# Dilated attention on one core: numerators and sums written in token order, sums first, fewer bias masks

## The chip, the cores and the metric

One core of a Trainium2 chip. The metric is the device time of one execution in microseconds. The kernel before takes 363.38 us (median of 3 runs, 363.35 to 364.58). "PE" is the tensor engine, "DVE" the vector engine, "ACT" the scalar engine, "POOL" GpSimd. PSUM is the memory of the tile `ps`, which the matmuls of every view below write to; the kernel lays it out as eight banks of 512 fp32 columns.

## The reference

Attention over 8 batches, 8 heads, 576 tokens, 64 columns a head. Heads 0 to 3 see a plain window of 32 tokens; heads 4 to 7 a dilated one, every fourth token back to 128. Then a gated feed-forward layer.

```python
rel = pos[:, None] - pos[None, :]
mask_plain = (rel >= 0) & (rel < 32)
mask_dil = (rel >= 0) & (rel < 32 * 4) & (rel % 4 == 0)
scores = np.where(masks, scale * q @ k.T, -1e9)
attn = softmax(scores)            # the kernel divides by the sums after attn @ v
x = (attn @ v)                    # to [4608 tokens, 512]
out = (gelu(x @ w_gate) * (x @ w_val)) @ w_out
```

## The kernel before

Work comes in 32 "units" of two heads: unit n is batch n // 4; n % 4 of 0 and 1 are plain, 2 and 3 dilated. The feed-forward layer runs in 9 blocks of 512 tokens, and the attention of later batches is placed between its matmuls by a list of places. Batches 2 (units 8 to 11) and 3 (12 to 15) are worked off within the output matmuls of blocks 1 and 2. In the dilated heads a token is 4i + 2m + s; the kernel keeps each class (m, s) apart.

```python
def emit_pv(n, b0, parts=("num", "den"), wide=False):
    ...                                        # dilated unit:
    for s in range(2):                         # numerators
        for m in range(3):
            for hl in range(2):
                h, p0 = 2 * hp + hl, (2 * s + hl) * DW
                if m < 2:
                    add(hl, 512 * s + m * NCL, run(P), vd[:, h, 2 * m + s, :], p0 + m * NCL, run(P), m == 0)
                else:
                    two = [[NCL, 2], [1, 16]]
                    add(hl, 512 * s + P, two, vr[:, h, s, :], p0 + P, two, False)
    ...                                        # sums: matmuls with ones, 192/96/96/192 columns (narrow), 288/288 (wide)

def norm_r(n, b0, wide=False):                 # DVE: transpose of the sums, reciprocal, transpose back
def norm_x(n, b0):                             # DVE: xT = numerators * reciprocals
    num = ps[:, b0 : b0 + 2, 0 : 2 * NCL].rearrange("p s (m i) -> p i m s", m=2)
    nc.vector.tensor_tensor(dst.rearrange("p (i m s) -> p i m s", m=2, s=2), num,
                            rb.rearrange("p (s m i) -> p i m s", s=2, m=2), ALU.mult)

def emit_s(n, b0, pe_mask=False):              # scores and exponential; if pe_mask, PE first adds a bias of -60000
    ...                                        # (4 matmuls) where the mask is 0; else DVE multiplies by the mask after
biased = (6, 7, 8, 9, 10, 11, 12, 13, 14, 15)
four = "1.5s 1.9v 1.12s 2.6v 2.12s 3.3v 3.12s 3.12v"   # places in blocks 1 and 2: tile.matmul, s = scores, v = values

def pv(last):                                  # what a "v" does
    n = todo.pop(0)
    emit_pv(n, V)                              # V: one set of three PSUM banks
    if not last:
        mask_next()                            # DVE mask of the NEXT unit, ahead of ...
    norm(n, V)                                 # ... the normalisation of this one
```

"Narrow" units (values within output matmuls) have three PSUM banks for numerators and sums together; "wide" ones have two for each.

The softmax here doesn't subtract the row's maximum and nothing guards it: scores larger than these inputs give would overflow.

## Time and profile before

| | before |
|---|---|
| time, median | 363.38 us |
| PE busy | 345.5 of a span of 362.5 us |
| DVE busy | 184.8 us |
| PE waits for DVE's products of dilated units (value matmuls + first feed-forward matmuls) | 2.0 + 1.6 us |
| product of a dilated unit / plain unit | 1126 / 745 ns |

The prediction below shows the lines that carry this. The chain that ended last (start us, length us, what) gives the length of a whole piece on PE: the bias of a plain unit (L323), of a dilated one (L346), and the numerators and sums of a narrow dilated unit (unit 18, 20 matmuls) and of a wide dilated one (unit 26, 16 matmuls):

```profile
94.97 0.57 PE ps L323 x4
98.37 0.49 PE ps L346 x4
181.76 0.66 PE ps L433 x20
238.43 0.65 PE ps L433 x16
```

The groups by line, for the numerators of the dilated units (busy us, mean ns | idle before):

```profile
L433 PE MATMUL ps<-P,vd 128*64 128x128 f16 x128 | 6.8, 224 | 2.0 <-DVE xT L469 2.0
L433 PE MATMUL ps<-P,vr 128*64 128x32 f16 x64 | 5.2, 179 | 0.0
```

A mean of 224 ns is the length of one pipelined matmul, not its cost: in the timeline of unit 10, printed in the prediction, two run side by side, in the two halves of the array (128*64 each, where a feed-forward matmul is 128*128): the 1152 columns of its numerators take 0.30 us (104.30 to 104.60), where one after the other they would make 0.48 at the 0.42 ns a column of a 512-column matmul (0.216 us). Four of 128 columns take 0.13 and 0.11 us there from their start to that of the next group, two of 32 columns 0.03 us. What a matmul costs is read from the start of one to the start of the next.

### The profile page before, as it was taken

Reading aid. Unit: us, or ns where it says so; the run is one execution under the profiler, and the core shown is the slowest. Engines: PE = TensorE matmul, PEld = TensorE weight load, DVE = VectorE, ACT = ScalarE, POOL = GpSimd, SP = SyncE. Lnnn points to the kernel's source line nnn. Section 1 sums busy time; section 2 is a strip of 40 time slices with the busy share of each in tenths; the row PEclk is TensorE's granted clock in tenths of the full one; section 3 lists DMA queues with packets and bytes.
Section 4 is the critical chain, followed back from the end, with each engine's and each line's share of the span. In section 5 each row is a group of like instructions: output and inputs, shape, how many; then the busy total and the mean of one; then the engine's idle time right before and its main releaser. Section 6 shows DMA issues by size and latency. Waiting matters only on the chain.

```text
span 362.5 us, 6061 instructions
## 1 busy us (share of the span) xinstructions
PE 345.5 (95%) x2400; PEld 164.2 (45%) x2400; DVE 184.8 (51%) x278; ACT 146.0 (40%) x212; POOL 78.2 (22%) x110
## 2 busy tenths in 40 slices
PE   7879899999989999899999999999999999999995
PEld 2554354444544445444444444444444444444442
DVE  1585445744266325864477638783669413303320
ACT  1733255253543345434553356336542223312321
POOL 2580333540432332063003410240000000000000
PEclk9899999999999999999999999999999999999999
DMA  7999999999899898599438962893100030011002
GB/s 184 244 177 214 220 133 194 192 157 235 188 142 204 181 161 154 136 173 135 101 93 186 158 96 89 195 140 72 60 30 2 0 116 2 1 60 58 0 29 89
DMA packets 107292, 45.31 MB, mean 125 GB/s; under 512 B 83040, under 2 KB 102496, under 8 KB 107264
## 3 DMA queue, kind: packets, MB, share of 16 engines
q1 hardware_dynamic: 84272, 31.21, 39.8%
q0 software_dynamic: 21456, 12.01, 26.6%
q10 hardware_dynamic: 1536, 1.70, 2.0%
q8 instruction: 19, 0.31, 0.4%
q14 instruction: 9, 0.07, 0.1%
HBM read 40.13 MB, written 9.44 MB: 137 GB/s over the span
## 4 chain that ended last, share of the span: by engine, by line
PE 78%; DMA 13%; DVE 5%; POOL 2%; ACT 1%; issue 1%; ACTq 0%; SPq 0%; POOLq 0%; DVEq 0%
PE ps L481 41%; PE ps L512 25%; PE ps L433 5%; DMA xT<-in_k_dram 4%; DMA st<-in_k_dram 3%; PE ps L493 3%; DMA wv<-in_moe_w_val_dram 3%; DMA wo<-in_moe_w_out_dram 2%; DVE xT L469 2%; PE ps L360 1%; DMA sv<-in_v_dram 1%; PE ps L330 1%; DVE dt L451 1%; DVE rb L455 1%; PE ps L346 1%; POOL qp L251 1%
## 5 line engine op out<-in xcount | busy, mean ns | idle before, releaser
L506 DVE SCALAR_TENSOR_TENSOR u_all<-g,ps 128x512 f16<-128x512 f16 x108 | 73.5, 686 | 85.9 <-PE ps L481 76.9
L505 ACT ACTIVATE g<-ps 128x512 f16<-128x512 f32 x108 | 63.6, 597 | 126.0 <-PE ps L481 115.0
L512 PE MATMUL ps<-wo,u_all 128*128 128x512 f16 x432 | 101.1, 380 | 1.1 <-DMA wo<-in_moe_w_out_dram 0.7
L481 PE MATMUL ps<-xT,wg 128*128 128x512 f16 x392 | 100.7, 379 | 0.3
L481 PE MATMUL ps<-xT,wv 128*128 128x512 f16 x392 | 100.6, 379 | 0.0
L512 PEld LDWEIGHTS <-u_all 128*128 128x128 f16 x432 | 39.2, 98 | 45.4 <-issue 1.5
L481 PEld LDWEIGHTS <-wv 128*128 128x128 f16 x392 | 38.4, 98 | 46.4 <-issue 0.2
L481 PEld LDWEIGHTS <-wg 128*128 128x128 f16 x392 | 37.2, 98 | 45.0 <-issue 2.1
L523 ACT ACTIVATE osb<-ps 128x512 f32<-128x512 f32 x33 | 19.7, 597 | 49.0 <-PE ps L512 49.0
L451 DVE STREAM_TRANSPOSE dt<-ps 128x576 f32<-128x576 f32 x32 | 24.9, 779 | 26.2 <-PE ps L433 25.9
L190 POOL CAST qp<-st 128x2048 f16<-128x2048 f32 x6 | 11.4, 1894 | 99.0 <-DMA st<-in_k_dram 84.8
L455 DVE STREAM_TRANSPOSE rb<-rc 128x576 f32<-128x576 f32 x32 | 24.9, 778 | 1.1
L362 ACT ACTIVATE P<-ps 128x1152 f16<-128x1152 f32 x16 | 18.1, 1130 | 10.8 <-PE ps L360 10.8
L340 ACT ACTIVATE P<-ps 128x960 f16<-128x960 f32 x16 | 15.5, 970 | 10.7 <-PE ps L330 10.6
L469 DVE TENSOR_TENSOR xT<-ps,rb 128x576 f16<-128x576 f32 x16 | 17.9, 1126 | 0.3
L493 PE MATMUL ps<-xT,wg 128*128 128x512 f16 x40 | 15.2, 379 | 2.1 <-DVE xT L469 1.6
L525 DVE TENSOR_SCALAR osb<-ps 128x512 f32<-128x512 f32 x3 | 2.1, 691 | 28.8 <-PE ps L512 28.8
L433 PE MATMUL ps<-P,ones 128*64 128x96 f16 (+5 forms) x216 | 14.3, 245 | 1.6 <-ACT P L362 1.6
L493 PE MATMUL ps<-xT,wv 128*128 128x512 f16 x40 | 15.2, 379 | 0.0
L466 DVE TENSOR_TENSOR xT<-ps,rb 128x576 f16<-128x576 f32 x16 | 11.8, 745 | 0.3
L370 DVE TENSOR_TENSOR P<-P,mask_p 128x1344 f16<-128x1344 f16 x10 | 8.4, 852 | 6.8 <-ACT P L341 6.8
L370 DVE TENSOR_TENSOR P<-P,mask_d 128x1152 f16<-128x1152 f16 x8 | 6.1, 757 | 11.1 <-ACT P L362 11.1
(75 smaller groups left out, 244.2 us busy)
## 6 DMA issues: line engine op xcount, KB each, us to landing
out_dram<-osb SPq DMA_DIRECT2D x36, 256.0 KB, 2.1
sv<-in_v_dram SPq DMA_DIRECT2D x40, 128.0 KB, 3.2
st<-in_q_dram SPq DMA_DIRECT2D x24, 128.0 KB, 3.7
st<-in_k_dram SPq DMA_DIRECT2D x24, 128.0 KB, 3.1
qd<-in_q_dram POOLq DMA_DIRECT2D x7, 256.0 KB, 5.0
qd<-in_k_dram POOLq DMA_DIRECT2D x7, 256.0 KB, 6.9
vd<-in_v_dram POOLq DMA_DIRECT2D x7, 256.0 KB, 7.2
wg<-in_moe_w_gate_dram POOLq DMA_DIRECT2D x3, 512.0 KB, 7.4
```

Of the source, the lines that this page charges most:

```text
L340: nc.scalar.activation(pt[:, :, 0:PB], sb[:, 0, :, 0:PB], AF.Exp, bias=0.0, scale=scale)
L362: nc.scalar.activation(pt, ps[:, b0 : b0 + 4, 0:DW], AF.Exp, bias=0.0, scale=scale)
L433: nc.tensor.matmul(o, lhs, rhs, start=st, stop=True, skip_group_check=True)
L451: nc.vector.transpose(dst, den)
L455: nc.vector.transpose(rb.rearrange("p (b c) -> p b c", c=32), bass.AP(tensor=rc.tensor, offset=rc.offset, ap=[rc.ap[0], [1, 18], [0, 32]]),)
L469: nc.vector.tensor_tensor(dst.rearrange("p (i m s) -> p i m s", m=2, s=2), num, rb.rearrange("p (s m i) -> p i m s", s=2, m=2), ALU.mult,)
L481: nc.tensor.matmul(ps[:, b0 + gi, :], w[:, kc, ns], xT[kc][:, tok], start=(kc == 0), stop=(kc == NKC - 1))
L493: nc.tensor.matmul(ps[:, pairs[nb] + gi, :], w[:, kc, ns], xT[kc][:, tok], start=(kc == 0), stop=(kc == NKC - 1),)
L505: nc.scalar.activation(g, ps[:, b0, :], AF.Gelu)
L506: nc.vector.scalar_tensor_tensor(u_all[:, nb, :], g, USCALE, ps[:, b0 + 1, :], ALU.mult, ALU.mult)
L512: nc.tensor.matmul(ps[:, bank, :], u_all[:, fc, tb * P : (tb + 1) * P], wo_t[fc // 4][:, fc % 4, :], start=(fc == 0), stop=(fc == NNB - 1),)
L523: nc.scalar.activation(osb, ps[:, bank, :], AF.Copy, bias=0.0, scale=1.0 / USCALE)
```

## The change

The intent is to relieve DVE: PE writes numerators and sums of dilated units straight in token order, so that DVE's product reads in order. With the DVE time won, six of ten bias masks move from PE to DVE, and the sums are issued before the numerators so that DVE can begin earlier.

```diff
-    def emit_pv(n, b0, parts=("num", "den"), wide=False):
+    def emit_pv(n, b0, parts=("den", "num"), wide=False):
 ...  # sums now ahead of numerators; dilated sums, for s in 0, 1:
-                    else ((0, 0, 192, 288), (0, 192, 96, 800), (1, 0, 96, 896), (1, 96, 192, 1312))
+                    for i0, i1 in ((0, P),) if wide else ((0, 16), (16, P)):
+                            add(hl, d0 + 4 * i0 + s, [[2, 2], [4, i1 - i0]], ones, p0, [[NCL, 2], [1, i1 - i0]], s == 0)
+                        add(hl, d0 + 512 + s, [[2, 2], [4, 16]], ones, p0, two, s == 0 and wide)
 ...  # dilated numerators
-            add(hl, 512 * s + m * NCL, run(P), vd[:, h, 2 * m + s, :], p0 + m * NCL, run(P), m == 0)
+            add(hl, 2 * m + s, [[4, P]], lhs, p0, run(P), m == 0 and s == 0)
-            add(hl, 512 * s + P, two, vr[:, h, s, :], p0 + P, two, False)
+            add(hl, 512 + s, [[2, 2], [4, 16]], vr[:, h, s, :], p0 + P, two, s == 0)
 ...  # product, all units
+        nc.vector.tensor_tensor(xT[hp][:, b * S : (b + 1) * S], psf[:, b0 * 512 : b0 * 512 + S], rb, ALU.mult)
-    biased = (6, 7, 8, 9, 10, 11, 12, 13, 14, 15)
-    four = "1.5s 1.9v 1.12s 2.6v 2.12s 3.3v 3.12s 3.12v"
+    biased = (6, 7, 8, 12)
+    four = "1.5s 1.6v 1.12s 2.4v 2.12s 3.3v 3.12s 3.12v"
```

An access pattern `[[4, P]]` means P elements, each four fp32 (16 bytes) from the last.

More of the change, by code (lines that the diff above doesn't have):

```diff
@@ L390, in run @@
             return [[1, n]]
+        two = [[NCL, 2], [1, 16]]
+        d0 = 1024 if wide else 960
         if is_plain(n):
-            if "num" in parts:
-                for j in range(5):
-                    for hl in range(2):
-                        lhs = vp[:, j, 2 * hp + hl, :] if j < 4 else vt[:, 2 * hp + hl, :]
-                        w = (PW, PW, PW, P, PT)[j]
-                        add(hl, j * P, run(w), lhs, hl * PH + j * PW - (32 if j == 4 else 0), run(w), j in (0, 4))
             if "den" in parts:
-                d0 = 1024 if wide else 960
                 groups = (
@@ L410, in emit_pv @@
                         add(hl, d0 + q0, [[P, runs], [1, w]], ones[:, 0:D], hl * PH + p0, [[PW, runs], [1, w]], st)
-        else:
+            if "num" in parts:
+                for j in range(5):
+                    for hl in range(2):
+                        lhs = vp[:, j, 2 * hp + hl, :] if j < 4 else vt[:, 2 * hp + hl, :]
+                        w = (PW, PW, PW, P, PT)[j]
+                        add(hl, j * P, run(w), lhs, hl * PH + j * PW - (32 if j == 4 else 0), run(w), j in (0, 4))
+        else:
+            if "den" in parts:
+                for s in range(2):
+                    for i0, i1 in ((0, P),) if wide else ((0, 16), (16, P)):
+                        for hl in range(2):
+                            dims = [[2, 2], [4, i1 - i0]]
+                            p0 = (2 * s + hl) * DW + i0
+                            add(hl, d0 + 4 * i0 + s, dims, ones[:, 0:D], p0, [[NCL, 2], [1, i1 - i0]], s == 0)
+                    for hl in range(2):
+                        p0 = (2 * s + hl) * DW + P
+                        add(hl, d0 + 512 + s, [[2, 2], [4, 16]], ones[:, 0:D], p0, two, s == 0 and wide)
             if "num" in parts:
@@ L417, in emit_pv @@
                             if m < 2:
-                                add(hl, 512 * s + m * NCL, run(P), vd[:, h, 2 * m + s, :], p0 + m * NCL, run(P), m == 0)
-                            else:
-                                two = [[NCL, 2], [1, 16]]
-                                add(hl, 512 * s + P, two, vr[:, h, s, :], p0 + P, two, False)
-            if "den" in parts:
-                groups = (
-                    ((0, 0, DW, 1024), (1, 0, DW, 1536))
-                    if wide
-                    else ((0, 0, 192, 288), (0, 192, 96, 800), (1, 0, 96, 896), (1, 96, 192, 1312))
-                )
-                for i, (s, c, w, c0) in enumerate(groups):
-                    for hl in range(2):
-                        add(hl, c0, run(w), ones[:, 0:D], (2 * s + hl) * DW + c, run(w), wide or i != 2)
+                                lhs, p0 = vd[:, h, 2 * m + s, :], p0 + m * NCL
+                                add(hl, 2 * m + s, [[4, P]], lhs, p0, run(P), m == 0 and s == 0)
+                            else:
+                                add(hl, 512 + s, [[2, 2], [4, 16]], vr[:, h, s, :], p0 + P, two, s == 0)
         for o, lhs, rhs, st in mms:
             nc.tensor.matmul(o, lhs, rhs, start=st, stop=True, skip_group_check=True)
-    def den_ap(n, b0, wide):
-        if is_plain(n):
-            c0, dims = (1024, [[1, S]]) if wide else (960, [[1, S]])
-        else:
-            c0, dims = (1024, [[512, 2], [1, 288]]) if wide else (288, [[512, 3], [1, 192]])
-        base = psf[:, b0 * 512 + c0 : b0 * 512 + c0 + 1]
-        return bass.AP(tensor=base.tensor, offset=base.offset, ap=[base.ap[0]] + dims)
     def norm_r(n, b0, wide=False):
         dt = nrm.tile([P, 18, 32], F32, tag="dt", bufs=1)
-        den = den_ap(n, b0, wide)
-        dims = den.ap[1:]
-        dst = dt.rearrange("p b c -> p (b c)")
-        if len(dims) == 2:
-            dst = dst.rearrange("p (x y) -> p x y", y=dims[1][1])
-        nc.vector.transpose(dst, den)
+        d0 = b0 * 512 + (1024 if wide else 960)
+        nc.vector.transpose(dt.rearrange("p b c -> p (b c)"), psf[:, d0 : d0 + S])
         rc = nrm.tile([P, 18], F32, tag="rc")
@@ L463, in norm_x @@
         rb = tiles.pop(("rb", n))
-        dst = xT[hp][:, b * S : (b + 1) * S]
-        if is_plain(n):
-            nc.vector.tensor_tensor(dst, psf[:, b0 * 512 : b0 * 512 + S], rb, ALU.mult)
-        else:
-            num = ps[:, b0 : b0 + 2, 0 : 2 * NCL].rearrange("p s (m i) -> p i m s", m=2)
-            nc.vector.tensor_tensor(
-                dst.rearrange("p (i m s) -> p i m s", m=2, s=2),
-                num,
-                rb.rearrange("p (s m i) -> p i m s", s=2, m=2),
-                ALU.mult,
-            )
+        nc.vector.tensor_tensor(xT[hp][:, b * S : (b + 1) * S], psf[:, b0 * 512 : b0 * 512 + S], rb, ALU.mult)
     def ffn1(c, nb, b0):
```

## The prediction

> **What bounds the kernel now.** I read the page first (busy time, then the slices), then the waits of PE, the windows by stage, the chain, and the timeline where PE waits.
>
> ```profile
> PE 345.5 (95%) x2400; PEld 164.2 (45%) x2400; DVE 184.8 (51%) x278; ACT 146.0 (40%) x212; POOL 78.2 (22%) x110
> PE ps L433 <- DVE xT L469: 2.0, 3, 1.1
> PE ps L433 <- ACT P L362: 1.6, 2, 0.8
> PE ps L493 <- DVE xT L469: 1.6, 3, 0.7
> 54.40:72.70 18.30, 18.30 (x163) 8.76 (x163) 12.30 (x18) 7.13 (x11) 8.86 (x11) 1.00 1.15 191
> 90.20:113.10 22.90, 21.32 (x205) 10.63 (x203) 11.77 (x18) 10.36 (x14) 8.85 (x12) 1.00 1.09 168
> 130.50:153.50 23.00, 21.79 (x216) 11.10 (x214) 12.62 (x19) 11.69 (x16) 3.09 (x5) 1.00 0.86 146
> ```
>
> In the windows the columns are length, then busy time of PE, PE loads, DVE, ACT, POOL. PE is the bound: in most stages it is busy all the time (18.30 of 18.30). It waits 1.58 us in the stage 90.2 to 113.1 and 1.21 us in 130.5 to 153.5, the ends of the two blocks that hold batches 2 and 3, and there it waits for DVE's normalisation of dilated units (L469). Before 54.4 us, transfers pace the kernel: PE waits 0.72 us there for a piece of the output weights. So anything that costs PE time after 54.4 us is paid in full, and DVE time is worth something only in those two stages, about 2.8 us in all.
>
> The costs that matter, from the groups (busy, mean ns), and one narrow dilated unit in the timeline (start, length):
>
> ```profile
> L469 DVE TENSOR_TENSOR xT<-ps,rb 128x576 f16<-128x576 f32 x16 | 17.9, 1126 | 0.3
> L466 DVE TENSOR_TENSOR xT<-ps,rb 128x576 f16<-128x576 f32 x16 | 11.8, 745 | 0.3
> L370 DVE TENSOR_TENSOR P<-P,mask_p 128x1344 f16<-128x1344 f16 x10 | 8.4, 852 | 6.8 <-ACT P L341 6.8
> L370 DVE TENSOR_TENSOR P<-P,mask_d 128x1152 f16<-128x1152 f16 x8 | 6.1, 757 | 11.1 <-ACT P L362 11.1
> L249 ACT COPY qTp<-ps 128x576 f16<-128x576 f16 x4 | 2.4, 634 | 1.0 <-PE ps L264 1.0
> 104.30 0.30 PE L433 MATMUL ps<-P,vd 128*64 128x128 f16 x4
> 104.43 0.18 PE L433 MATMUL ps<-P,vr 128*64 128x32 f16 x2
> 104.46 0.28 PE L433 MATMUL ps<-P,vd 128*64 128x128 f16 x4
> 104.57 0.18 PE L433 MATMUL ps<-P,vr 128*64 128x32 f16 x2
> 104.60 0.42 PE L433 MATMUL ps<-P,ones 128*64 128x192 f16 x8
> 104.95 2.12 PE L512 MATMUL ps<-wo,u_all 128*128 128x512 f16 x9
> 105.06 0.78 DVE L451 STREAM_TRANSPOSE dt<-ps 128x576 f32<-128x576 f32 x1 [0.99 <-PE ps L433]
> 108.18 0.30 PE L433 MATMUL ps<-P,vd 128*64 128x128 f16 x4 [1.10 <-DVE xT L469]
> ```
>
> Twelve numerator matmuls start within 104.30 to 104.60[...], although those with 128 columns need 53 ns each at the rate of the feed-forward matmuls (512 columns in 0.216 us): the two halves of the array run side by side[...]. The last two lines show the wait: DVE starts on the sums at 105.06, and PE gets the banks back at 108.18.
>
> [...] the ACT copy to qTp reads PSUM at steps of 192 bytes and takes 634 ns for 576 columns, while contiguous reads by ACT (597 ns for 512 columns, 1130 for 1152, thus 0.83 ns a column) would take about 650. [...]
>
> **The change, part by part.**
>
> *Bias masks removed.* Units 9, 10, 11, 13, 14, 15 lose their four bias matmuls. The chain gives 0.57 us for a plain unit's four and 0.49 for a dilated one's: 2 x 0.57 + 4 x 0.49 = 3.1 us of PE. In exchange DVE gets 2 x 0.85 + 4 x 0.76 = 4.7 us of mask products, all in the two stages where PE already waits for DVE.
>
> *Faster normalisation.* The dilated product now reads both operands in order, so 1126 becomes about 745 ns: 16 x 0.38 = 6.1 us less DVE.
>
> *More, smaller matmuls.* The instruction order of both builds shows the dilated sums going from 8 to 12 matmuls in the narrow form (units 10, 11, 14, 15, 18, 19, 22, 23, 27) and from 4 to 8 in the wide one (2, 3, 6, 7, 26, 30, 31); PE has 24 matmuls less and 64 more. [...] Numerators unchanged.
>
> *Steps of 16 bytes.* All dilated numerators and sums now write every fourth fp32 element[...] So +0.54 us for a narrow unit and +0.52 for a wide one, taking the place of the +0.13 and +0.07.
>
> *Sums first.* In the wide form sums and numerators lie in different banks, so DVE can start some 0.3 us earlier, but those units are not the ones waited for. In the narrow form the last numerators share a bank with the sums. In the changed build the narrow product has no wait for PE of its own, while the wide one has: the wait in front of the sums' transpose already covers the numerators. Nothing is gained in batches 2 and 3.
>
> *Stage of batch 2, step by step, on the clock of before, steps free.* Scores of unit 9 end at 95.37 (no bias before them), its exponential takes 1.37 (as now, 95.94 to 97.31): 96.74. Values of unit 8 run 95.6 to 96.3. But DVE's queue has unit 9's mask ahead of unit 8's normalisation: mask to 97.6, then 2.75 for transpose, reciprocal, transpose, product: 100.4. PE has only 10 output matmuls and one set of scores until unit 9's values, ready at 99.3: it waits 1.1. Unit 9's values end at 101.1; the mask of 10 is done at 101.15, normalisation of 9 at 103.9; PE comes at 104.3 and does not wait. Values of 10 end at 105.1; the mask of 11 waits for its exponential (104.7) and ends at 105.5; normalisation of 10 ends at 108.2; PE has nine matmuls and is ready at 107.1: waits 1.1. Values of 11 end at 109.1, normalisation at 111.8, and the last four matmuls of the next block's start go at 111.9, against 112.05 now. So the 1.55 us of bias matmuls in this stage comes back as about 0.15. At half rate it is 0.27 later instead. Batch 3 is alike.
>
> *Sums after 54.4 us.* Free steps: block 0 +0.14 (units 6, 7), batches 2 and 3 -0.15 each, blocks 3 to 6 +0.26, +0.26, +0.20, -0.06 (two wide units, less a 0.2 us wait for a dilated product near 278 that goes): +0.5 us, 363.9. Half rate: +1.04, +0.27, +0.27, +1.08, +1.08, +1.06, +0.84: +5.6 us, 369.0. The start gains some 0.3 from faster products, hidden behind the later transfers.
>
> **Rivals.** (a) Steps are free and DVE is no limit: then 3.1 us of bias, the two stages' waits of 2.8, less 1.5 for added matmuls, would make about 359. For it: a lighter DVE overall. Against: DVE's balance in the two stages is four products x 0.38 less, six masks 4.7 us more, and the masks stand in front of normalisations. (b) Free steps, DVE as the new wait: 363.9. For it: the order of the DVE queue. [...] (c) Half rate: 369.0[...]. (d) A quarter of the rate[...]: about 1.4 us a unit, 381. Against: ACT's lone reads at 0.83 ns. Someone re-tuned the places of the values (1.6 and 2.4 for 1.9 and 2.6), which suggests that a gain was expected; it keeps (a) and (b) alive.
>
> **Range and chances.** I give (c) 0.55, (b) with a bit of (a) 0.33, (d) 0.12. The middle of that mixture is some 368.0 us; the tenth and ninetieth parts are about 362.8 and 371.5. Slower by 2% means above 370.65: all of (d) and the upper end of (c), 0.2. Faster by 2% means under 356.1, more than (a) gives: 0.01. Within 2%: 0.79.
>
> **What would show it.** Narrow dilated units at 1.2 us of PE rather than 0.66 to 0.71, wide ones likewise, mean matmul times for 128 columns up by some 50 ns: half rate right. Around 0.8 us: free. The product of dilated units near 745 ns. PE's waits for DVE in the two stages up to about 2.5 us each (free steps) from 1.6 and 1.2, among them a new one before unit 9's and 13's values. I would be wrong if stepped writes are free and PE nevertheless loses no time behind the new masks[...].

Passages that no trace of this case shows are cut from it, and with them terms of its sum. With free steps these came to +0.13 us for the sums of a narrow dilated unit (386 for 260 ns) and +0.07 for those of a wide one (314 for 240 ns, the latter from the timeline of before, 24.27 to 24.51); the block sums above hold them, in all +0.5 us, 363.9. At half rate they came to +0.23 us for the numerators, +0.31 for the narrow sums (574 for 260 ns) and +0.29 for the wide ones (527 for 240 ns), hence the +0.54 and +0.52 us a unit, in all +5.6 us, 369.0. The sums took 0.42 ns for a contiguous column (0.216 us for 512) and, as the author's estimate, 0.83 ns for a stepped one, taken over from ACT's reads (597 ns for 512 columns, 1130 for 1152); for small matmuls they took a least time that no trace shows. That PE's writes keep to half rate was not shown either before the change ran.

## The result and the profile after

The changed kernel takes 368.02 us (median of 4 runs, 367.35 to 369.74) beside 363.55 us of the kernel before in the same rounds. The ratio is 1.0124, 95% interval 1.0085 to 1.0164: 1.2% slower. Ratios here are the mean time of one kernel's fast runs over that of the other's of the same rounds, so not quite the ratio of the medians quoted. (The 363.38 us above is the median of three earlier runs of the kernel before.)

The lines of code moved: L433 of before is L435, L469 is L453, L451 is L440, L512 is L491. First the same group view as above, of the changed kernel:

```profile
L453 DVE TENSOR_TENSOR xT<-ps,rb 128x576 f16<-128x576 f32 x32 | 23.8, 752 | 2.1 <-PE ps L435 1.4
L435 PE MATMUL ps<-P,vd 128*64 128x128 f16 x128 | 10.0, 295 | 0.0
L435 PE MATMUL ps<-P,vr 128*64 128x32 f16 x64 | 7.7, 234 | 0.0
```

The product of dilated units now takes what a plain one takes (one group of 32, 752 ns). The numerators are longer: 295 for 224 ns, 234 for 179. The timeline shows what that costs PE. One narrow dilated unit, sums first:

```profile
181.69 0.69 PE L435 MATMUL ps<-P,ones 128*64 128x32 f16 x12
182.21 0.39 PE L435 MATMUL ps<-P,vd 128*64 128x128 f16 x4
182.39 0.24 PE L435 MATMUL ps<-P,vr 128*64 128x32 f16 x2
182.46 0.39 PE L435 MATMUL ps<-P,vd 128*64 128x128 f16 x4
182.64 0.24 PE L435 MATMUL ps<-P,vr 128*64 128x32 f16 x2
```

The sums take 0.52 us from start to start. Half the numerators, 182.21 to 182.46, take 0.25 us; they are 128 + 128 + 32 columns in each half of the array, so 0.87 ns a column. The same half took 0.15 us before (0.16 and 0.14 in unit 10). The chain gives the whole pieces of the same two units, 18 and 26:

```profile
181.76 1.12 PE ps L435 x24
239.69 1.11 PE ps L435 x20
```

So a narrow dilated unit went from 0.66 to 1.12 us and a wide one from 0.65 to 1.11: +0.46 each. As a check, PE's busy time from the start of block 3's output matmuls to that of block 6's, with eight dilated units in it, rose from 112.67 to 116.11 us, 0.43 a unit.

In the stage of batch 2, DVE's queue shows the masks ahead of the normalisations (timeline; in brackets the idle time before and what ended it):

```profile
96.18 0.86 DVE L370 TENSOR_TENSOR P<-P,mask_p 128x1344 f16<-128x1344 f16 x1 [5.77 <-ACT P L341]
96.95 0.78 DVE L440 STREAM_TRANSPOSE dt<-ps 128x576 f32<-128x576 f32 x1
98.94 0.76 DVE L453 TENSOR_TENSOR xT<-ps,rb 128x576 f16<-128x576 f32 x1
99.75 0.49 PE L435 MATMUL ps<-P,ones 128*64 128x64 f16 x10 [0.84 <-DVE xT L453]
107.76 0.69 PE L435 MATMUL ps<-P,ones 128*64 128x32 f16 x12 [0.74 <-DVE xT L453]
97.88 1.02 PE L491 MATMUL ps<-wo,u_all 128*128 128x512 f16 x4 [0.31 <-ACT osb L502]
```

Unit 8's values ended at about 95.7, but its normalisation starts at 96.95, behind unit 9's mask, which itself waited for its exponential. PE then waits 0.84 us at 99.75 for banks that it did not wait for before. The last line is a second new wait, of which there is another at 103.05 (0.32 us): PE has finished the scores of a dilated unit and waits until ACT has copied the finished outputs (`osb`) out of their bank. In the kernel before, the bias matmuls stood in that place (98.21 to 98.79, while ACT copied from 98.41 to 99.01), so a part of their time seems to have been hidden behind the copy; e1_steps, which keeps all the bias matmuls, does not have these two waits. The windows of the two stages (length, then busy PE, loads, DVE, ACT, POOL):

```profile
89.45:112.81 23.36, 21.02 (x201) 10.81 (x200) 13.25 (x21) 10.30 (x14) 8.86 (x12) 1.00 1.13 179
130.24:153.44 23.20, 21.25 (x210) 11.03 (x209) 14.01 (x22) 11.38 (x16) 3.09 (x5) 1.00 0.61 121
```

PE's idle time there rose from 1.58 to 2.34 us and from 1.21 to 1.95 us, although three bias masks had gone from PE in each.

To leave out the start, which is paced by transfers (PE waits 3.4 us for them in the trace of before, all before 54.4 us) and differs from one trace to the next (the last of those waits ends at 54.39 us before, at 52.51 after), I also measure a stretch in each trace: from the first feed-forward matmul of block 1 to the first output matmul of the last block. Before it is 347.98 - 69.03 = 278.95 us; after 350.71 - 68.43 = 282.28, +3.33. Block 0, from the output weights' arrival to that point, went from 14.64 (54.39 to 69.03) to 15.92 (52.51 to 68.43), +1.28. Together +4.6, and the medians differ by 4.5.

### The profile page after: what moved, and what is told of

Read it like the earlier page. It is cut to its first block, busy times and chain, and to the rows that moved or that the text cites. A ratio compares the mean times of both kernels' runs of the same rounds, so it can differ in the third digit from the quotient of the medians.

```text
span 365.2 us, 6145 instructions
## 1 busy us (share of the span) xinstructions
PE 351.0 (96%) x2440; PEld 169.4 (46%) x2440; DVE 182.7 (50%) x284; ACT 145.6 (40%) x212; POOL 78.3 (21%) x110
## 4 chain that ended last, share of the span: by engine, by line
PE 73%; DMA 13%; DVE 6%; SPq 3%; POOL 1%; ACT 1%; issue 1%; ACTq 0%; DVEq 0%; POOLq 0%
PE ps L460 40%; PE ps L491 22%; PE ps L435 7%; DMA xT<-in_k_dram 3%; DMA st<-in_k_dram 3%; PE ps L472 3%; DMA wv<-in_moe_w_val_dram 3%; SPq L185 2%; DMA wo<-in_moe_w_out_dram 2%; DMA sv<-in_v_dram 2%; DVE rb L444 2%; DVE dt L440 1%; DVE xT L453 1%; PE ps L330 1%; PE ps L360 1%
## 5 line engine op out<-in xcount | busy, mean ns | idle before, releaser
L491 PE MATMUL ps<-wo,u_all 128*128 128x512 f16 x432 | 101.1, 380 | 1.8 <-ACT osb L502 1.6
L491 PEld LDWEIGHTS <-u_all 128*128 128x128 f16 x432 | 39.3, 97 | 46.5 <-issue 2.1
L440 DVE STREAM_TRANSPOSE dt<-ps 128x576 f32<-128x576 f32 x32 | 24.9, 779 | 14.3 <-PE ps L435 14.3
L453 DVE TENSOR_TENSOR xT<-ps,rb 128x576 f16<-128x576 f32 x32 | 23.8, 752 | 2.1 <-PE ps L435 1.4
L435 PE MATMUL ps<-P,ones 128*64 128x32 f16 (+6 forms) x280 | 19.3, 274 | 4.4 <-DVE xT L453 2.8
L370 DVE TENSOR_TENSOR P<-P,mask_p 128x1344 f16<-128x1344 f16 x12 | 10.5, 879 | 18.4 <-ACT P L341 18.4
L435 PEld LDWEIGHTS <-ones 128*64 128x64 f16 x280 | 11.6, 117 | 17.3 <-issue 14.6
L370 DVE TENSOR_TENSOR P<-P,mask_d 128x1152 f16<-128x1152 f16 x12 | 9.1, 756 | 13.3 <-ACT P L362 13.3
```

Of the source, the lines that this page charges most:

```text
L370: nc.vector.tensor_tensor(pt, pt, mb, ALU.mult)
L435: nc.tensor.matmul(o, lhs, rhs, start=st, stop=True, skip_group_check=True)
L440: nc.vector.transpose(dt.rearrange("p b c -> p (b c)"), psf[:, d0 : d0 + S])
L453: nc.vector.tensor_tensor(xT[hp][:, b * S : (b + 1) * S], psf[:, b0 * 512 : b0 * 512 + S], rb, ALU.mult)
L491: nc.tensor.matmul(ps[:, bank, :], u_all[:, fc, tb * P : (tb + 1) * P], wo_t[fc // 4][:, fc % 4, :], start=(fc == 0), stop=(fc == NNB - 1),)
```

## The experiments

Eleven kernels ran, five rounds each; the runs of before taken beside them had medians of 363.76, 364.37 and 364.22 us in three groups. "Stretch" is the difference against 278.95 us, from one trace each.

| kernel | median us | ratio, 95% interval | stretch us |
|---|---|---|---|
| the change | 368.02 | 1.0124 (1.0085 to 1.0164) | +3.33 |
| e1_steps | 368.20 | 1.0117 (1.0100 to 1.0135) | +3.16 |
| e3_contig | 362.79 | 0.9966 (0.9945 to 0.9988) | -0.06 |
| e4_pairs | 362.99 | 0.9974 (0.9960 to 0.9989) | -0.98 |
| e5_step2 | 369.10 | 1.0137 (1.0114 to 1.0159) | +3.93 |
| e2_masks | 365.20 | 1.0028 (1.0000 to 1.0055) | +0.54 |
| e6_sums_first | 364.16 | 1.0012 (0.9978 to 1.0045) | -0.34 |
| e7_first_units | 363.30 | 0.9969 (0.9951 to 0.9988) | -1.21 |
| e8_early | 362.15 | 0.9944 (0.9923 to 0.9965) | -2.19 |
| e9_two_masks | 361.91 | 0.9940 (0.9916 to 0.9964) | -2.82 |
| e10_product | 366.24 | 1.0060 (1.0045 to 1.0074) | +1.94 |
| e11_both | 363.48 | 0.9984 (0.9969 to 0.9999) | +0.04 |

### e1_steps: the stepped writes alone

```diff
 # the changed kernel, with before's order, masks and places
-    parts=("den", "num")
+    parts=("num", "den")
-    biased = (6, 7, 8, 12)
+    biased = (6, 7, 8, 9, 10, 11, 12, 13, 14, 15)
-    four = "1.5s 1.6v 1.12s 2.4v 2.12s 3.3v 3.12s 3.12v"
+    four = "1.5s 1.9v 1.12s 2.6v 2.12s 3.3v 3.12s 3.12v"
```

> The kernel before with only the stepped writes and the plain product (masks, places of the values and numerators-first as before). Theory (a stepped write costs twice a contiguous one): narrow dilated units take 1.1 us of PE rather than 0.66 to 0.71, wide ones 1.1 rather than 0.70, 14 units after 54 us make +6.0 us; the product's 0.38 us less comes off the waits at the end of the two blocks, about -0.76 each, so about +4.3 us in all: 367 to 368.5. Rival (the masks on DVE cost the time, steps little): within 1 us of before.

Correct; 368.20 us, ratio 1.0117. The stepped writes and the product alone make nearly all of the result. PE's waits for the products of DVE fell to 1.1 us in all (two waits; before, 2.0 and 1.6), as the shorter product would have it. The units grew as in the changed kernel (1.12 and 1.11 us), and that is more.

### e3_contig, e4_pairs, e5_step2: what about the step costs

All three are the changed kernel with the same matmuls; only the columns that they write to differ, and the result is wrong.

```diff
 # e3_contig: neighbouring columns
-    add(hl, 2 * m + s, [[4, P]], ...)
+    add(hl, (2 * m + s) * P, run(P), ...)
 # e4_pairs: two neighbours, then a step to the eighth column
+    add(hl, 2 * (2 * m + s), [[8, 64], [1, 2]], ...)
 # e5_step2: every second column
+    add(hl, 256 * m + s, [[2, P]], ...)
 # (the rest numerators and the sums likewise)
```

> The changed kernel with the same matmuls, writing to neighbouring columns (result wrong on purpose). Theory of the steps: narrow and wide dilated units near 0.8 us of PE; some of what PE gains in batches 2 and 3 turns into waiting for DVE; 363.5 to 365. Rival (the number of small matmuls, 64 more, is the cost): stays at 367 to 368.5.

362.79 us, ratio 0.9966: the time comes back, so the number of matmuls was not the cost. The chain of e3_contig has the narrow dilated unit back at 0.71 us with its 24 matmuls (0.66 with the 20 of before):

```profile
181.94 0.71 PE ps L436 x24
```

Its stretch (-0.06) is spoiled by one disturbance: a mask product of 1.95 us in place of 0.86 in the profiled execution; PE then waited 1.93 us for the product behind it, where e4_pairs waits 1.02. I have no cause for it.

> The changed kernel writing two neighbouring columns, then a step of eight (result wrong on purpose). [...] as e3_contig within 0.7 us, dilated units near 0.8 us of PE. Rival (any pattern that is not contiguous[...], slows a matmul): as the changed kernel, 367 to 368.5, units 1.1 us.

362.99 us, as e3_contig within 0.2. One narrow unit in the timeline of e4_pairs:

```profile
180.10 0.49 PE L435 MATMUL ps<-P,ones 128*64 128x32 f16 x12
180.44 0.28 PE L435 MATMUL ps<-P,vd 128*64 128x128 f16 x4
180.59 0.28 PE L435 MATMUL ps<-P,vd 128*64 128x128 f16 x4
```

Half the numerators take 0.15 us, as before; in e3_contig they take 0.14 (182.21 to 182.35). In this run a pattern that is not contiguous cost nothing; it filled two neighbouring fp32 columns at a time. The sums of a wide unit, in matmuls of 256 columns, also take 0.30 to 0.31 us in e3_contig and e4_pairs alike. (Every pair began at an even column; a pair that begins at an odd one was not run.)

> The changed kernel with steps of 8 bytes in place of 16 (result wrong on purpose). [...] as slow as the changed kernel, units 1.1 us of PE, 367 to 368.5. [...]

369.10 us, as slow as the change. (The rival was that a step of 8 bytes costs less than one of 16: 363.5 to 365 us.) In the timeline of e5_step2:

```profile
184.34 0.69 PE L436 MATMUL ps<-P,ones 128*64 128x32 f16 x12
184.87 0.39 PE L436 MATMUL ps<-P,vd 128*64 128x128 f16 x4
185.12 0.39 PE L436 MATMUL ps<-P,vd 128*64 128x128 f16 x4
```

These are the changed kernel's intervals: 0.53 and 0.25 us. A step of 8 bytes costs what one of 16 does. A column that was written without its neighbour took 0.87 ns in both, twice the 0.42 of a contiguous one (from the 0.216 us of a 512-column matmul). All three runs fit this, and the rivals (matmul count, any pattern that is not contiguous, a step of 8 bytes cheaper than one of 16) each fail at one of them.

### e2_masks: the masks and places alone

```diff
 # the kernel before
+    biased = (6, 7, 8, 12)
+    four = "1.5s 1.6v 1.12s 2.4v 2.12s 3.3v 3.12s 3.12v"
```

> The kernel before with only the new list of bias masks and the new places of the values. Theory: the 3.1 us of bias matmuls that go come back as waits behind the masks in DVE's queue; the last four matmuls of the block of batch 2 start 21.9 to 22.4 us after the block's scores, against 21.8 now; total -0.3 to +1.0 us. Rival (PE is the bound and the bias matmuls are plain PE time): -2.5 to -3.1 us, about 360.6.

365.20 us, ratio 1.0028 (1.0000 to 1.0055): 3.1 us of PE work removed and nothing gained. From the start of block 1's output matmuls to the start of block 2's takes 40.65 us against 40.32. The timeline of e2_masks shows where the bias time went:

```profile
99.52 0.45 PE L433 MATMUL ps<-P,vp 128*64 128x160 f16 x8 [0.91 <-DVE xT L466]
107.61 0.30 PE L433 MATMUL ps<-P,vd 128*64 128x128 f16 x4 [1.27 <-DVE xT L469]
111.48 0.38 PE L493 MATMUL ps<-xT,wg 128*128 128x512 f16 x1 [0.46 <-DVE xT L469]
```

The first wait is new; the second grew from 1.10. With the two waits for ACT's copies (0.32 and 0.31), which are new here too and which e1_steps does not have, they make up for the bias matmuls. The last four matmuls of this stage start at 111.48, 22.3 us after its first bias matmul (89.16); in the kernel before it is 22.0 us (90.06 to 112.05). The expectation had put them 0.1 to 0.6 us later.

### e6_sums_first: the order alone

```diff
 # the kernel before: the two parts of emit_pv exchanged
-    parts=("num", "den")
+    parts=("den", "num")
```

> The kernel before with only the order changed, sums ahead of numerators. Theory: narrow units share banks, so the transpose of the sums still waits for all matmuls, and wide ones aren't waited for: within 0.4 us of before, PE's waits for DVE at the ends of the two blocks as before (1.6 and 1.2 us). Rival: each narrow normalisation starts 0.3 us earlier, the two blocks lose about 0.6 us each, -1 us or more.

Ratio 1.0012 (0.9978 to 1.0045). PE's waits in the block of batch 2 are 1.11 and 0.49 us, as before (1.10 and 0.45). In the timeline of e6_sums_first the transpose of a narrow unit's sums starts after the last numerators, not after the sums:

```profile
104.34 0.44 PE L433 MATMUL ps<-P,ones 128*64 128x192 f16 x8
104.88 0.18 PE L433 MATMUL ps<-P,vr 128*64 128x32 f16 x2
105.10 0.78 DVE L451 STREAM_TRANSPOSE dt<-ps 128x576 f32<-128x576 f32 x1 [0.97 <-PE ps L433]
```

(The other numerators, between the first two of these lines, are left out.) The order alone does nothing that these rounds can see.

### e7_first_units, e8_early, e9_two_masks: masks where DVE is idle

If a mask costs only where it stands ahead of a normalisation for which PE waits, other units should be chosen.

```diff
 # e7_first_units: the kernel before with
+    biased = (6, 7, 9, 10, 11, 13, 14, 15)
 # e8_early: also
+    four = "1.1s 1.3v 1.12s 2.1v 2.9s 2.12v 3.12s 3.12v"
 # e9_two_masks: as e8_early, but
+    biased = (6, 7, 10, 11, 14, 15)
+    four = "1.1s 1.5v 1.12s 2.3v 2.9s 2.12v 3.12s 3.12v"
```

> The kernel before with masks by DVE for units 8 and 12 alone, whose masks fall where DVE is idle for 3 us or more. Theory (a mask costs only where it stands ahead of a normalisation that PE waits for): the 2 x 0.57 us of bias matmuls are saved in full, -1.1 us. Rival (any mask moved to DVE comes back as waiting): within 0.4 us of before.

363.30 against 364.37 us, ratio 0.9969, stretch -1.21: the 1.1 us in full. The change had left exactly these two units biased.

> As e7_first_units, with the values of batches 2 and 3 begun some 13 output matmuls earlier. Theory (from the first values to the end of the block the chain of four normalisations, 13.8 us, sets the end; its start does): the waits of 1.6 and 1.2 us at the ends of the blocks fall under 0.7 us each; with the bias matmuls saved -3 to -4.5 us, about 359.5. Rival (PE waits at the first values for unit 8's mask and exponential instead): -1 us or less.

362.15 us, ratio 0.9944, stretch -2.19: less than I expected. In the timeline of e8_early one wait for DVE is left in the block of batch 2:

```profile
111.03 0.38 PE L493 MATMUL ps<-xT,wg 128*128 128x512 f16 x1 [0.45 <-DVE xT L469]
```

The wait before unit 11's values, 1.10 us in the kernel before, is gone. The wait before the last four matmuls stays, because twelve feed-forward matmuls (2.6 us) cannot cover a normalisation of 3.1 us (107.93 to 110.98), wherever the chain began. Block 1 to block 2 took 39.09 us for 40.32; 0.57 of that is bias. Block 2 to block 3 gave 0.34 us, where I had expected its wait of 1.2 us to fall under 0.7.

> As e8_early, with the masks of units 9 and 13 on DVE too, their scores early enough that mask and exponential are over when the first values end, and the values a few matmuls later. Theory: two times 0.57 us of bias matmuls go, about 0.1 us each comes back: -0.9 us against e8_early, so -3 us against before, ratio 0.992. Rival (these masks delay the first normalisation as in the changed kernel): no faster than e8_early.

361.91 us against 364.22, ratio 0.9940, stretch -2.82: correct and the fastest of all, faster than both kernels. Against e8_early, run on another chip, the ratios do not tell a difference; the stretch is 0.63 shorter, somewhat less than expected. Block 1 to block 2 now takes 38.66 us with PE busy for 37.70.

### e10_product, e11_both: another way to a fast product

Here PE writes contiguously, and DVE reads in order and writes with a step instead.

```diff
 # the kernel before (e10) and e9_two_masks (e11)
-    num = ....rearrange("p s (m i) -> p i m s", m=2)
-    dst.rearrange("p (i m s) -> p i m s", ...), rb.rearrange("p (s m i) -> p i m s", ...)
+    num = ....rearrange("p s (m i) -> p s m i", m=2)
+    dst.rearrange("p (i m s) -> p s m i", ...), rb.rearrange("p (s m i) -> p s m i", ...)
```

> The kernel before with only the dilated product walked in the order of the sums and numerators, so that it reads in order and writes fp16 with a step of 8 bytes. Theory (the product's extra 0.38 us is the stepped reading): 1126 falls to about 750 ns with no stepped PE write; the waits of PE at the ends of the two blocks fall from 1.6 and 1.2 us to about 0.8 and 0.5; -1.3 to -1.7 us, ratio about 0.996. Rival (a step costs DVE the same on either side): 1.1 us a product, time as before.

The theory fell: 366.24 us against 364.22, ratio 1.0060. The group of the product in e10_product:

```profile
L469 DVE TENSOR_TENSOR xT<-ps,rb 128x576 f16<-128x576 f32 x16 | 22.7, 1444 | 0.3
```

1444 ns: writing fp16 with a step of 8 bytes costs more than stepped reading (1126), and in order costs 751. PE's waits for that product, over the whole execution, rose from 2.0 and 1.6 us to 3.1 and 2.2.

> e9_two_masks and e10_product together. Theory: the wait left before the last four matmuls of the next block's start (0.45 us in e8_early) goes to about 0.1: -0.6 us against e9_two_masks, ratio about 0.990. Rival: with the first values begun early PE waits little for the product, so no more than e9_two_masks.

363.48 us, ratio 0.9984, slower than e9_two_masks (361.91) in the same rounds. The loss of e10_product carries over: PE waits 3.4 us for products there (1.4 for those of plain units, 1.1 and 0.9 for those of dilated ones), against 0.7 in e9_two_masks.

## Why the prediction was right, point by point

**The rate of a stepped write.** The prediction gave half the contiguous rate a chance of 0.55. All that the trace of before had for it is ACT's reads of PSUM: 634 ns for 576 columns with a step of 192 bytes. That was an analogy: it is a read, by another engine, whose contiguous reads take 0.83 ns a column too (about 650 ns for 576). The rest of its ground was not shown by a trace. The measured rate of PE's stepped writes is 0.87 ns a column; e3, e4 and e5 together show that it holds for steps of 8 and 16 bytes (0.25 us for half the numerators), and not where neighbouring pairs are filled (0.15 us). This was the step on which the result hung.

**Its size.** Predicted +0.54 and +0.52 us a unit, measured +0.46 for both. The term that was too large is that of the small matmuls: the sum gave each small pair a time of its own (no trace shows it), beside the columns of the larger ones. That makes 0.57 us for the narrow sums and 0.53 for the numerators; the timeline has 0.52 and 0.50, and since the 576 columns alone make 0.48 at the predicted 0.83 ns, little is left for the small pairs. The same mistake made the added matmuls dear: predicted +0.13 and +0.07 us, while e3 shows 0.71 and 0.67 us for a narrow and a wide unit, 0.05 and 0.02 more than before. How small and large matmuls add up in a group is not shown exactly: from start to start, two numerator matmuls of 32 columns took 0.03 us in the timeline of before and 0.07 in that of after. The rival "steps free" thus came out 0.8 to 1.0 us under before (e3 and e4, in the same rounds), where the prediction had it 0.5 us above; a wait named under "The sum by blocks" is another part of that.

**The bias masks.** Right in what the masks are worth, and in their place in DVE's queue. The new wait before unit 9's values was put at 1.1 us (0.84 measured) and the whole stage 0.27 us later at half rate; from block 1's output matmuls to block 2's it was +0.30 (40.62 for 40.32), from block 2's to block 3's +0.29 (40.87 for 40.58). With the steps made free, e4_pairs has -0.23 and -0.41 (40.09 and 40.17), predicted -0.15 each. e2_masks shows the loss with no stepped write. What the prediction did not see is the waits for ACT's copies, 0.31 and 0.32 us of the 2.34 us that PE is idle in the first stage.

**Sums first.** Right for narrow units: no gain, by e6_sums_first. For wide units the earlier start shows in the changed kernel: for unit 26 the transpose of the sums starts at 240.40, the last numerators at 240.56. No run shows a gain from it.

**The sum by blocks.** Predicted +5.6 us after the start, found +4.6. Block 0: +1.28 for +1.04; PE waited 0.3 us for a mask product there that took 1.16 rather than 0.86. Blocks 3 to 6: 4.06 predicted; from the start of block 3's output matmuls to that of the last, before 347.98 - 172.02 = 175.96, after 350.71 - 172.01 = 178.70, +2.74. Of the 1.3 us between, 0.8 is the unit's size: PE's busy time grew by 3.44 us for the eight dilated units of these blocks, where 4.26 had been predicted (the 4.06, and 0.2 for a wait that was to go and went). The other 0.5 is a wait that the prediction did not count: it was there before, at 187.25, and is not now, as PE is busy with unit 19's longer matmuls at that time. It is in the waits of the kernel before:

```profile
PE ps L493 <- ACT P L340: 0.5, 1, 0.5
```

**The product.** 752 ns as predicted; worth little, because only four of sixteen are waited for in the two stages.

**The median.** 368.0 predicted, 368.02 measured; this is luck, since the number is the middle of a mixture of cases. The case that came true had been put at 369.0. The mixture is loose besides: the chances with 369.0, 363.9 and 381 give 368.8, lower only by the share of (a), which is not stated, and the 381 of case (d) is not worked out (14 units by 1.4 us would make 383).

**Left open.** The start: the weights that PE waits for in block 0 came 1.9 us earlier in the profiled run after (52.51 for 54.39). In e3_contig and e4_pairs, whose transfers are those of the changed kernel, they came at 54.24 and 53.34, and the four runs of the changed kernel differ by 2.4 us. I did not find what decides it.

## What to carry to other kernels

Before giving PE a permuted output, look at pairs of neighbouring fp32 columns: here, where a matmul filled both at a time, a step was free (0.15 us for half the numerators in e4_pairs, as before), and where it did not, its columns took twice the time (0.87 ns for 0.42). A saving on an engine that is seldom waited for did not pay that back. Where work moves from the bound engine to another, ask what stands behind it in that engine's queue: moving a mask was worth the full 0.57 us of its bias matmuls where DVE was idle and the mask stood ahead of no normalisation that PE waited for (e7). And look at what the removed work had been hiding: here, it seems, a part of the time in which ACT copied a bank. Compare stretches of the trace as well as times when the start varies.
